# A backward FFT's blocks turned by TensorE or by DMA: two of seven blocks change sides

## The chip, the cores and the metric

The kernel runs on one core of one Trainium2 chip. The metric is the time of one execution on the device in microseconds (us), as the median of several runs. A core has a matrix engine (PE), a vector engine (DVE), a scalar engine (ACT), a general engine (POOL), a queue engine that issues transfers (SP), and 16 DMA engines that carry the transfers out.

## The reference, shortened

A network of four layers and all its gradients: two long-convolution layers (A), each followed by a dense layer with a silu (B). The vector-Jacobian product gives nine outputs: the result and the gradients of A_q, A_k, A_v, A_shift_k, A_ssm_k, A_ssm_D, B_w1 and B_w2.

```
def _A_ref(q, k, v, shift_k, ssm_k, ssm_D):          # S = 2048, D = 448
    k_shift = sum of k shifted by 0..3 rows, times shift_k
    kv = k_shift * v
    y = irfft(rfft(kv padded to 2S) * rfft(ssm_k padded to 2S))[:S]
    return q * (y + kv * ssm_D)

def _B_ref(x, w1, w2):                               # F = 1792
    return silu(x @ w1) @ w2

x = A_q
x = x + _A_ref(_layernorm(x), k, v, shift_k, ssm_k, ssm_D)
x = x + _B_ref(_layernorm(x), w1, w2)
x = x + _A_ref(_layernorm(x), k, v, shift_k, ssm_k, ssm_D)
x = x + _B_ref(_layernorm(x), w1, w2)
# outputs: x, and the gradients of the eight inputs named above, for grad_out
```

Both A layers share k, v and the filter, so the gradient of the convolution's output, summed over the two layers, goes through one FFT. Its product with the spectrum of the filter leads to the gradients of k, v and shift_k, and its product with the spectrum of kv to those of ssm_k and ssm_D.

## The kernel before

**Stages.** A prefix (`_ssm_prefix`) computes the spectra of the filter and of kv and the convolution's output y. The main part (`Main.run`) walks over four chunks of 512 rows and runs both dense layers forward and backward. The suffix (`_ssm_suffix`, from about 510 us) takes the summed gradient through the FFT and back.

**The FFT in two stages.** A length of 4096 is split into 128 by 16 by two parts. Stage 1 (`_s1_gy`, `_fft_stage1`, L218) multiplies with a table for each of 16 residues n2 and casts the result into `A1g`, 128 partitions (frequencies) by 14336 columns (channel pairs, real and imaginary part, n2). Stage 2 needs those columns on the partitions. So `A1g`, seen as `A1f` with 112 tiles of 128 x 128, is turned tile by tile into `B1v`, in seven blocks `Z[0]` to `Z[6]` of 16 tiles (2048 columns) each. This is the loop that the change touches.

**How a block is turned before.** For each of its 16 tiles, `_turn64` makes two transposes on TensorE (L225), one for each half of 64 partitions, into a bank `ps_tr` of the two PSUM banks with the tag "mm". Then one copy of 128 x 2048 brings the block to `Z[g]`; `bal.pick` gives it to ACT (L116) or DVE (L117), by the load that it has booked on each. After each block `jobs.run(1)` puts in four matmuls of the jobs.

**The jobs.** The gradients of w1 and w2 are products over all 2048 rows: 28 column blocks (14 of each), each with two groups of 16 matmuls (`ps_d`, L1046), one for each dense layer. Their stationary operands were written to memory by the main part (`a_d`, `g_d`) and come back by `Jobs.load` (L1038): one transfer of 512 KB on SP's queue for each group into `dstat`, which has four slots. `Jobs.run(n)` takes n steps of four matmuls. The jobs are spread over the suffix by hand, so that TensorE has work beside the FFT. `jobs.last_ld` is the load issued last as the program is written down.

**What follows the loop.** `spectrum(cp)` runs stage 2 (L236) over block cp, casts the result back over `Z[cp]` (L1199) and copies it with its halves swapped (L276). `inverse(cp)` multiplies with the two spectra, which `spec_load` brings by POOL's queue (L1180, L1181; tiles `kk_d` and `wts`), runs the inverse stage 2 (L265) and writes over `A1g` (as `B1k`) and over `B1v`. Steps are in the order spectrum 0, spectrum 1, inverse 0, spectrum 2, and so on. Then come the inverse stage 1 (L1271, L1300) and the sums for k, v and shift_k (L1257 to L1262, L1322, L1325).

**What sets the order.** TensorE's order is that of the program (`manual_schedule`). On the other engines and queues a scheduler places the instructions; `tc.issue_after(x)` asks that what is inside stands behind x. SP's queue issues strictly in its order: a transfer that waits holds up all behind it.

**Transposes by DMA already there.** `dma_start_transpose` turns on the way. In the prefix it turns two of seven blocks of the filter's first stage (L426, from `KAB` to `KAB`), and weights (L436, L437). In the main part it turns the jobs' operands before they are stored (L595, tile `turned`, 16 or 12 tiles at a time).

Of the kernel before, what the change touches and what calls it, by code (L numbers as in the profile page):

```python
# [11 lines left out]
BF16 = mybir.dt.bfloat16  # L12
# [5 lines left out]
P = 128  # L18
# [95 lines left out]
def _copy(nc, eng, out, in_):  # L114
    if eng is nc.scalar:
        return nc.scalar.copy(out, in_)  # L116
    return eng.tensor_copy(out, in_)  # L117
# [18 lines left out]
def kernel(  # L136
# [63 lines left out]
    with tc.manual_schedule(engines={nc.tensor.engine}):  # L200
        with ExitStack() as es:
            Main(k, es).run(ys)
        _ssm_suffix(k)
# [18 lines left out]
def _turn64(k, pt, i, src):  # L222
    for r in range(2):
        rs = slice(64 * r, 64 * r + 64)
        k.nc.tensor.transpose(pt[:, r, i, :], src[rs], k.ident[rs, rs])  # L225
# [920 lines left out]
def _ssm_suffix(k):  # L1146
    nc, tc, bal = k.nc, k.tc, k.bal
    jobs = k.jobs
    k_pm = _pm(k.A_k[0])
    v_pm = _pm(k.A_v[0])  # L1150
    psum = k.psum
    mm = dict(tag="mm", bufs=2)
    k.pt = dict(s1=mm, s2=mm, v=mm)
    A1 = k.A1g
    with ExitStack() as es:
# [12 lines left out]
        Z = [B1v_[:, 16 * g:16 * g + 16, :] for g in range(7)]  # L1168
# [3 lines left out]
        A1f = A1[:].rearrange("p a c n s -> p (a c n s)").rearrange("p (a b) -> p a b", b=P)  # L1172

        def spec_load(cp):
            lo, hi = cp * 2048, (cp + 1) * 2048
            if cp % 2:
                kk = [kk1[:, i] for i in range(2)]
            else:
                kk = [sp.tile([P, 2048], BF16, name="kk_d", tag="gK", bufs=2)[:] for i in range(2)]
            nc.gpsimd.dma_start(out=kk[0], in_=k.SPEC_d["K"][:, lo:hi])  # L1180
            k.last_sp = nc.gpsimd.dma_start(out=kk[1], in_=k.SPEC_d["KV"][:, lo:hi])  # L1181
            return kk

        kks = [spec_load(0)]
        for g in range(7):
            pt = psum.tile([P, 2, 16, 64], BF16, name="ps_tr", **mm)
            for i in range(16):
                _turn64(k, pt, i, A1f[:, 16 * g + i, :])
            _copy(nc, bal.pick(2048, dve_ns=0.53), Z[g].rearrange("p i (r x) -> p r i x", r=2), pt[:])
            jobs.run(1)  # L1190
        kks.append(spec_load(1))

        def spectrum(cp):
# [181 lines left out]
```

## Time and profile before

| what | value |
|---|---|
| three runs | 702.48 us median (701.94 to 702.93) |
| the profiled execution | 701.8 us, its span 700.0 us |
| PE busy in the span | 666.0 us (95%) |
| DVE, ACT, POOL busy | 484.1, 432.9, 101.3 us |
| granted PE clock, mean | 0.998 |
| seven blocks turned, L225 | 224 transposes, 515.7 to 524.7 us, 190 ns each (they overlap) |
| their copies | four on DVE at 1224 ns, three on ACT at 1866 ns |
| job loads, L1038 | 56 of 512 KB, median 5.2 us from issue to landing |

The span is the time from the first to the last instruction of the profiled execution, 1.8 us less than its time. Busy time of PE is a sum over matmuls that are pipelined. "Idle before" names the time for which an engine stood ahead of an instruction, and the work that ended the wait. A chain of waits is the work that ended last, followed back from the end; where it stays on one engine without a pause, that engine sets the time there.

### The profile page before, as it was taken

The page shows a single profiled execution, that of the slowest core. Times are in us where ns is not written, and L with a number is a line of the kernel's source. Part 1 is how long each engine was busy: PE and PEld are TensorE (multiplying, and loading weights), DVE is VectorE, ACT ScalarE, POOL GpSimd, SP SyncE. Part 2 cuts the span into 40 slices and gives each one's busy share as a digit, 9 for nine tenths or more (in the row PEclk, how much of TensorE's full clock was granted, in tenths as well). Part 3 has the DMA queues.
Part 4 walks back from the last instruction along what each step waited for, and adds up shares of the span by engine and source line. Part 5 has one row for each costly group of instructions (what it writes and reads, how often), then busy time and mean ns, then how long its engine had stood idle before and what let it go on. Part 6 is the DMA issues. An engine that isn't in the chain of part 4 may idle for free.

```text
span 700.0 us, 14553 instructions
## 1 busy us (share of the span) xinstructions
PE 666.0 (95%) x5897; PEld 358.8 (51%) x5933; DVE 484.1 (69%) x1131; ACT 432.9 (62%) x522; POOL 101.3 (14%) x173
## 2 busy tenths in 40 slices
PE   6898789999999999999999999999999999999996
PEld 5876545454444444434444444544554555555664
DVE  6688862676889948899578874853946545538991
ACT  5888766968856857769577585223554553554431
POOL 1057110110011100111000100010111211102311
PEclk9999999999999999999999999999999999999999
DMA  8999938459899976698677799959557888966981
GB/s 321 270 298 306 376 84 210 118 107 243 219 231 249 246 200 166 146 240 221 185 165 194 194 242 329 262 172 229 177 208 280 307 279 307 352 188 215 331 293 42
DMA packets 199798, 161.03 MB, mean 230 GB/s; under 512 B 147698, under 2 KB 180213, under 8 KB 198963
## 3 DMA queue, kind: packets, MB, share of 16 engines
q1 hardware_dynamic: 184550, 111.78, 58.8%
q0 software_dynamic: 10368, 36.29, 15.3%
q10 hardware_dynamic: 4812, 12.04, 5.0%
q8 instruction: 46, 0.75, 0.4%
q14 instruction: 22, 0.17, 0.1%
HBM read 66.05 MB, written 54.60 MB: 172 GB/s over the span
## 4 chain that ended last, share of the span: by engine, by line
PE 57%; DVE 22%; issue 10%; ACT 5%; POOL 3%; DMA 2%; POOLq 0%; DVEq 0%; ACTq 0%
PE ps_d L1046 19%; PE ps_n L836 8%; PE ps_h L638 6%; PE ps_g L638 6%; PE ps_o L798 5%; DVE ln_st L301 2%; DVE lb_v L994 2%; PE ps_v L265 2%; PE ps_cv L449 2%; POOL rstd L306 2%; DVE n L309 1%; DVE lb_v L997 1%; DVE lb_v L998 1%; DVE X L802 1%; PE ps_h L642 1%
## 5 line engine op out<-in xcount | busy, mean ns | idle before, releaser
L1046 PEld LDWEIGHTS <-dstat 128*128 128x128 bf16 x896 | 84.0, 98 | 77.8 <-issue 4.0
L836 PE MATMUL ps_n<-w1T,ghT 128*128 128x448 bf16 x448 | 96.6, 353 | 2.0 <-DVE ghT L821 1.7
L798 PE MATMUL ps_o<-w2sb,aT 128*128 128x448 bf16 x448 | 89.2, 353 | 0.7 <-DVE X L802 0.7
L638 PE MATMUL ps_h<-nT,w1sb 128*128 128x512 bf16 (+1 forms) x410 | 83.5, 336 | 2.2 <-ACT Dall L116 1.0
L116 ACT CAST ghT<-ps_g 128x1024 bf16<-128x1024 f32 (+1 forms) x54 | 48.4, 899 | 58.4 <-PE ps_g L642 47.7
L638 PE MATMUL ps_g<-nT,w2T 128*128 128x512 bf16 x317 | 77.9, 379 | 2.2 <-DVE Dall L117 0.5
L836 PEld LDWEIGHTS <-ghT 128*128 128x128 bf16 x448 | 41.4, 98 | 50.7 <-DVE ghT L821 6.7
L798 PEld LDWEIGHTS <-aT 128*128 128x128 bf16 x448 | 43.2, 98 | 41.1 <-issue 2.8
L638 PEld LDWEIGHTS <-w1sb 128*128 128x128 bf16 x420 | 39.2, 98 | 36.7 <-issue 7.2
L781 ACT ACTIVATE aT<-ps_h 128x1024 bf16<-128x1024 f32 (+1 forms) x48 | 44.2, 921 | 19.4 <-PE ps_h L638 10.5
L116 ACT CAST Dall<-ps_h 128x1024 bf16<-128x1024 f32 (+2 forms) x60 | 54.3, 904 | 0.0
L994 DVE SCALAR_TENSOR_TENSOR lb_v<-lb_u,n 128x448 bf16<-128x448 bf16 x60 | 37.2, 620 | 24.6 <-ACT lb_u L840 24.1
L791 ACT ACTIVATE Dall<-Dall 128x1024 bf16<-128x1024 bf16 (+1 forms) x48 | 53.2, 1186 | 0.1
L638 PEld LDWEIGHTS <-w2T 128*128 128x128 bf16 x336 | 31.3, 98 | 42.1 <-issue 7.2
L306 POOL TENSOR_TENSOR rstd<-ln_ve,mhalf 128x2 f32<-128x2 f32 (+1 forms) x24 | 19.9, 831 | 221.1 <-DVE ln_ve L305 221.1
L1046 PE MATMUL ps_d<-X,dstat 128*128 128x448 bf16 x224 | 47.9, 353 | 0.0
L1046 PE MATMUL ps_d<-go,dstat 128*128 128x448 bf16 x224 | 47.2, 353 | 0.0
L1046 PE MATMUL ps_d<-n3m,dstat 128*128 128x448 bf16 x224 | 46.4, 353 | 0.0
L1046 PE MATMUL ps_d<-n1m,dstat 128*128 128x448 bf16 x224 | 46.3, 353 | 0.0
L840 ACT ACTIVATE lb_u<-ps_n,rstd 128x448 bf16<-128x448 f32 x32 | 20.5, 640 | 28.7 <-PE ps_n L836 24.3
L116 ACT CAST A1g<-ps_v 128x1024 bf16<-128x1024 f32 x14 | 14.9, 1066 | 36.5 <-PE ps_v L265 36.5
L802 DVE TENSOR_TENSOR X<-X,ps_o 128x448 bf16<-128x448 bf16 x32 | 19.5, 610 | 21.3 <-PE ps_o L798 21.1
(206 smaller groups left out, 1111.6 us busy)
## 6 DMA issues: line engine op xcount, KB each, us to landing
dstat<-a_d SPq DMA_DIRECT2D x28, 512.0 KB, 5.0
dstat<-g_d SPq DMA_DIRECT2D x28, 512.0 KB, 5.2
a_d<-turned SPq DMA_DIRECT2D x16, 512.0 KB, 3.0
g_d<-turned SPq DMA_DIRECT2D x16, 512.0 KB, 3.2
a_d<-turned SPq DMA_DIRECT2D x16, 384.0 KB, 2.7
g_d<-turned SPq DMA_DIRECT2D x16, 384.0 KB, 3.0
spec_K<-KAB POOLq DMA_DIRECT2D x7, 512.0 KB, 5.4
KAB<-KAB POOLq DMA_DIRECT2D x28, 128.0 KB, 4.6
```

The source lines that it names most:

```text
L116: return nc.scalar.copy(out, in_)
L265: nc.tensor.matmul(pv[:, r ^ (ci & 1), i, :], lhsT=src[ri, i * P:(i + 1) * P], rhs=k.Gsb[ri, g, ri], start=first, stop=not first)
L306: nc.gpsimd.tensor_tensor(out=r[:, lo:hi], in0=ve[:, lo:hi], in1=k.mhalf[:, lo:hi], op=ALU.pow)
L638: self.nc.tensor.matmul(ps, lhsT=w[:, b, ft * P:(ft + 1) * P], rhs=x[:, b], start=(start and b == 0), stop=(stop and b == bs[2]))
L781: self.last_silu = nc.scalar.activation(aT[hh][:, o:o + hi - lo, :], ps(lo, hi), ACT.Silu)
L791: self.nc.scalar.activation(dT[hh][:, o:o + n, :], dT[hh][:, o:o + n, :], ACT.Derivative_silu)
L798: nc.tensor.matmul(po[:, :D], lhsT=aT[ft // 7][:, ft % 7, tl * P:(tl + 1) * P], rhs=self.w2sb[:, ft, :], start=(ft == 0), stop=(ft == NF - 1))
L802: self.last_o = nc.vector.tensor_tensor(out=X[:, t, :], in0=X[:, t, :], in1=po[:, :D], op=ALU.add)
L836: nc.tensor.matmul(pn[:, :D], lhsT=gh[ft // 7][:, ft % 7, tl * P:(tl + 1) * P], rhs=self.w1T[:, ft, :], start=(ft == 0), stop=(ft == NF - 1))
L840: nc.scalar.activation(u0[:], pn[:, :D], ACT.Identity, scale=k.rstd[2 * L + 1][:, t:t + 1], accum_out=cp[:, tl, 0:1])
L994: nc.vector.scalar_tensor_tensor(out=v[:], in0=u0, scalar=-1.0 / D, in1=n_t, op0=ALU.mult, op1=ALU.mult, accum_out=cp[:, 1:2])
L1046: self.nc.tensor.matmul(ps[:, :D], lhsT=st[:, t, :], rhs=mov[:, t, :], start=(first and t == 0), stop=(last and t == NT - 1))
```

## The change

Blocks 0 to 4 are turned by TensorE as before. Blocks 5 and 6 are turned by one DMA transpose each, on SP's queue, straight from `A1g` to `B1v`, without a PSUM bank and without a copy. Block 5's is written ahead of the loop. Block 6's is written behind the fourth step of the loop, inside an `issue_after` on the job load written down last. The seven calls of `jobs.run(1)` stay. Nothing else of the kernel is changed.

```
+        def turn_dma(g):
+            nc.sync.dma_start_transpose(out=Z[g], in_=A1f[:, 16 * g:16 * g + 16, :].rearrange("p a b -> p (a b)"))
+
+        turn_dma(5)
         for g in range(7):
-            pt = psum.tile([P, 2, 16, 64], BF16, name="ps_tr", **mm)
-            for i in range(16):
-                _turn64(k, pt, i, A1f[:, 16 * g + i, :])
-            _copy(nc, bal.pick(2048, dve_ns=0.53), Z[g].rearrange("p i (r x) -> p r i x", r=2), pt[:])
+            if g < 5:
+                pt = psum.tile([P, 2, 16, 64], BF16, name="ps_tr", **mm)
+                for i in range(16):
+                    _turn64(k, pt, i, A1f[:, 16 * g + i, :])
+                _copy(nc, bal.pick(2048, dve_ns=0.53), Z[g].rearrange("p i (r x) -> p r i x", r=2), pt[:])
             jobs.run(1)
+            if g == 3:
+                with tc.issue_after(jobs.last_ld.ins):
+                    turn_dma(6)
         kks.append(spec_load(1))
```

## The prediction

> **What bounds the kernel now.** I read the windows table first, by stages around the edit. Columns: window, its length, busy time (and instructions) of PE, PEld, DVE, ACT, POOL, then the granted clock, DMA share and GB/s.
>
> ```profile
> 515.00:529.00 14.00, 14.00 (x279) 7.62 (x278) 4.97 (x5) 7.48 (x7) 0.79 (x2) 1.00 0.49 173
> 529.00:600.00 71.00, 71.00 (x923) 38.33 (x921) 42.61 (x66) 33.05 (x39) 12.72 (x20) 1.00 0.86 308
> 633.00:660.00 27.00, 27.00 (x190) 15.78 (x189) 26.23 (x40) 12.14 (x18) 8.88 (x15) 1.00 0.81 265
> 660.00:680.00 20.00, 20.00 (x169) 12.78 (x168) 20.00 (x28) 8.76 (x15) 4.15 (x7) 1.00 0.97 343
> ```
>
> PE is busy in all of each window, the edit's own (515 to 529) among them, at full granted clock: the job matmuls (ps_d, L1046) fill every gap, so PE time taken out moves everything behind it up. In the edit's window DVE has 4.97 us of work and ACT 7.48 of 14, so the copies that go with the turns bound nothing. DVE is full as well from 660 to 680; that is a rival below.
>
> Second, the chain of waits through the edit (start, length, work):
>
> ```profile
> 520.03 0.57 PE ps_tr L225 x32
> 520.60 0.86 PE ps_d L1046 x4
> 521.47 0.57 PE ps_tr L225 x32
> 522.04 0.86 PE ps_d L1046 x4
> 522.90 0.57 PE ps_tr L225 x32
> 523.48 0.86 PE ps_d L1046 x4
> 524.34 0.57 PE ps_tr L225 x32
> ...
> 527.85 3.13 PE ps_d L1046 x16
> ...
> 531.53 6.16 PE ps_d L1046 x32
> ```
>
> The chain stays on PE here, without a wait: one block's 32 small transposes, four job matmuls, the next block.
>
> Third, the timeline, for what stands before and behind the two new transfers (start, length, engine, line, work, idle time before and its releaser):
>
> ```profile
> 514.29 0.94 ACT L116 CAST A1g<-ps_s 128x896 bf16<-128x896 f32 x1
> 515.65 0.64 PE L225 MATMUL ps_tr<-ident,A1g 64*128 64x64 bf16 x32
> ...
> 518.62 0.32 SPq L1038 DMA_DIRECT2D dstat<-a_d  x1
> 524.37 0.32 SPq L1038 DMA_DIRECT2D dstat<-a_d  x1
> ...
> 532.23 3.19 PE L1046 MATMUL ps_d<-go,dstat 128*128 128x448 bf16 x16
> ...
> 538.32 1.07 ACT L116 CAST A1g<-ps_v 128x1024 bf16<-128x1024 f32 x1 [4.33 <-PE ps_v L265]
> ```
>
> A1g is complete at 515.23 (514.29 + 0.94). The job load issued at 518.62 refills the slot of the group that has just ended (the last `go` matmuls before 518.6). There are four slots, so it is first read four groups later: X from 519.10, go from 524.85, X from 528.54, then the go group at 532.23.
>
> Last, the DMA rows for transposes of just this size (128 rows by 2048 columns) and for job loads: what, and us from issue to landing; for the second row, ns that the queue held each (least/median/most).
>
> ```profile
> turned<-ghT SPq DMA_TRANSPOSE x1, 5.5
> L426 SPq DMA_TRANSPOSE KAB<-KAB x2: 3603/4920/6238, 20.2 to 26.5; - x2
> KAB<-KAB SPq DMA_TRANSPOSE x1, 10.4
> DMA to landing us min/median/max: 3.4/5.2/11.2
> ```
>
> The first row is the 16-tile transpose issued at 482.72, the third the first of the two in the prefix, and the last stands for all 56 job loads (L1038).
>
> **The change, part by part.**
>
> *Removed on PE: blocks 5 and 6.* A block with its four matmuls starts every 1.437 us ((524.27 - 515.65) / 6 in the timeline). Four job matmuls undisturbed take (6.16 - 3.13) / 16 x 4 = 0.757 us. So a block costs 0.68 us, and two cost **1.36 us**. From above: the busy row of 0.64 plus the 0.10 by which the four matmuls behind a turn are longer (0.86 against 0.757) gives 0.74, or 1.48 for two. I take 1.36 since it is the distance between starts. All of it is on the path.
>
> *Removed on DVE and ACT:* one copy of 1.22 us (DVE) and one of 1.87 us (ACT). Neither engine bounds the window: nothing gained. The load balancer's later choices are the same in the changed program; every later engine order is the same but for these rows.
>
> *Moved forward:* PE's first spectrum matmul (L236 at 527.22) comes 1.36 us sooner. It needs block 0, copied by 517.6, and the two "mm" banks, whose last users are now block 3 (DVE copy from 520.64, 1.23) and block 4 (ACT copy from 522.08, 1.87, done at 523.95). All are done before 525.9: no wait.
>
> *Added on SP: two transposes, next to each other.* The label says the second stands behind a job's load. The load meant is the one issued at 505.91 for the group that starts at 519.10; in the changed program's SP queue the loads of 510.07 and 513.86 come next, then both transposes, then the load of 518.62. The first transpose waits for the last cast into A1g (515.23) and for stores that read the memory B1v now takes, the latest being out_dram<-g of POOL at 509.82, landed about 3 us later. No load is due on SP between 513.86 and 518.62, so nothing stands behind that wait.
>
> *What the transposes hold up.* The pair at 482.72 held SP for 4.95 us, so here SP would be free at 515.3 + 5.0 = 520.3 and the load of 518.62 issues 1.7 us late. The second transpose, issued at about 518.7, lands at about 524.2 with 5.5 us; the load behind it lands at about 524.2 + 3.4 = 527.6 even if nothing of the two overlaps. PE now wants it at 532.23 - 1.36 = 530.87: 3.2 us to spare, **cost 0**. The other end is the prefix pair: 6.24 us of queue, so the second is issued at 521.5, lands at 531.9 (10.4), the load at 535.3, and PE stands for 4.4 us. The prefix pair ran behind some MB of input loads in its own queue (v_n lands 14.5 us after its issue), whereas here the DMA share is 0.67 from 516 to 520 and 0.31 from 520 to 524. The pair at 482.72 is the nearer row, since it ran among job loads like these, at a share of 1.08. The next load (524.37, now 523.7) is wanted three us after the first and has the same room.
>
> The Trainium skill ("VectorE: DVE Perf Modes", section "The three transpose paths" and the rules after it) speaks against the edit: a 128x128 transpose goes to TensorE where PSUM will do, with 390 ns there against 1309 ns by DMA. By that figure, 16 tiles one after the other are an estimated 20.9 us a block; the trace disagrees, with 5.5 us for 16 tiles above and 0.64 us on PE.
>
> *Readers of the result.* Blocks 5 and 6 are first read by the spectrum steps of chunks 5 and 6, after 580: cover of over 50 us. The first writer over A1g is the cast at 538.32, now 536.96; it now waits for both transposes to have read it, 12 us after 524.2, and even the dear end (531.9) is earlier. The kk_d loads on POOL's queue (issued 510.62 and 511.60, landing after 6.3 and 6.8) are wanted by DVE at 528.92, now 527.6: some 9 us of cover against sharing with the transposes.
>
> *Sum.* 700.0 - 1.36 + 0 = 698.6 us of span. The profiled execution took 701.8; the median shown is 702.48, 0.68 above it, so **701.1 us**, 0.19% less.
>
> **The rivals.**
>
> *Slower: the job loads starve.* Place: SP's ring between 515.3 and the go group at 530.87. For it: the prefix rows; transposes of this size have held the queue for 6.24 us. Against it: the shares, and PE busy in full (5.60 of 5.60) during the pair at 482.72. Price at the dear end 4.4 - 1.36 = 3.0, so 705.5. It decides once that load lands after 530.87, and the kernel is slower from 532.23 on.
>
> *Given back at the tail: DVE.* For it: DVE is full from 660 to 680.
>
> ```profile
> 630.63 0.62 DVE L1274 TENSOR_TENSOR gks<-gkv,gks 128x896 bf16<-128x896 bf16 x1 [7.77 <-ACT gkv L1273]
> 683.35 0.19 DVE L1325 SCALAR_TENSOR_TENSOR skjunk<-ps_sk,mask 128x32 bf16<-128x32 f32 x1 [0.97 <-PE ps_sk L1322]
> ```
>
> That chain begins after 7.77 us of idleness, on a cast that follows PE, so it moves up with PE; at its end DVE waits another 0.97 for PE. Were it not to move at all, 1.36 - 0.97 = 0.39 would be lost at most: 701.5.
>
> *The transposes run tile after tile.* The mechanism: a transpose's tiles serialise at twice the dear end's 10.4 us or more, so the load behind the second lands after 515.3 + 41.6 + 3.4 = 560.3 and PE stands for 29 us: 730. No transpose of the trace supports it; the larger ones of w2T land in 11.7 (median of two). The page above would put it there (41.9 us for two blocks by its figure, an estimate).
>
> *It doesn't do what it says.* The second transpose isn't held back as the label has it (above). As no load sits between, that costs nothing by itself and belongs to the forecast.
>
> **How the numbers follow.** Forecast 0.76; starved loads 0.16; tail 0.06; tile after tile 0.02. What a measurement of this kernel can tell from no change is about 0.2%, 1.4 us, and the forecast's 1.36 to 1.48 straddles it; I put 0.50 of its 0.76 beyond the line, since what the readings leave out can only add to the gain (in the timeline most turns show 0.37 us of issue idle before their first weight load, 0.7 for two, which overlaps the matmuls before it and is counted at nothing), and 0.26 within. With the tail within: faster 0.50, same 0.32, slower 0.18. The likeliest case's own range is 700.5 to 701.7 (a gain of 2.0 with those gaps, and of 0.8 if a load is a little late). For 8 in 10 it reaches toward the tail and a part of the starved case, up to a full give-back: 700.4 to 702.6.
>
> **What would show it.** Right: 64 fewer L225 transposes of A1g, the first L236 at about 525.9, PE full from 515 to 692, two transposes on SP at 515 to 519 landing by 525, the load behind them by 528. Wrong: PE idle ahead of the go group near 531 with a dstat load as the releaser; ACT's cast into A1g near 537 waiting for a transfer; PE earlier at 526 but not at 692.

## The result, and the profile after

The changed kernel takes 701.65 us in the median of 22 runs, the kernel before 702.87 us in 22 runs beside it: 1.2 us less, a ratio of 0.9983 (95% interval 0.9976 to 0.9990). Two later comparisons on the chip gave 0.9968 (0.9953 to 0.9984) and 0.9986 (0.9977 to 0.9994). So the change is worth 0.1 to 0.3%, about what such a comparison can just tell from nothing.

The profiled execution has a span of 699.5 us, against 700.0. That 0.5 is no measure of the change: in this execution the first turn of the loop starts at 516.46, 0.81 us later than before (515.65), and nothing ahead of it was changed. In the executions profiled for this study that start lies anywhere between 515.50 and 519.26. So I measure from the loop's first turn onward, where the three profiles of the changed kernel agree to a few hundredths (the kernel before has one profile). The windows of the changed kernel, with columns as before; they end 1.4 us sooner than those before, each on its own execution's clock:

```profile
515.00:527.60 12.60, 12.60 (x215) 6.67 (x213) 3.67 (x3) 5.48 (x6) 1.10 (x2) 1.00 1.09 258
527.60:598.60 71.00, 71.00 (x922) 38.42 (x921) 42.67 (x66) 33.94 (x40) 12.18 (x20) 1.00 0.87 311
658.60:678.60 20.00, 20.00 (x178) 13.00 (x176) 20.00 (x28) 9.29 (x16) 4.17 (x7) 1.00 0.97 337
```

PE is still busy in all of each window at full clock. The DMA share in the edit's window has gone from 0.49 to 1.09: the transfers fill what was half empty. The chain of waits through the edit (start, length, work):

```profile
521.41 0.86 PE ps_d L1046 x4
522.28 0.57 PE ps_tr L225 x32
522.85 3.89 PE ps_d L1046 x20
526.74 0.56 PE ps_s L236 x8
527.30 3.13 PE ps_d L1046 x16
```

The last turn is now followed by 20 job matmuls in one piece, with the two turns gone from between them, and then by the first spectrum matmuls. From the timelines: first turn to first spectrum matmul 526.67 - 516.46 = 10.21 us, before 527.22 - 515.65 = 11.57. That is 1.36 us. First turn to the last matmul of the program (ps_r, which starts at 694.38 and before at 694.89): 177.92 against 179.24. So 1.32 of the 1.36 is still there at the end.

What the transfers did, first in the timeline of the changed kernel:

```profile
516.11 7.43 SPq L1186 DMA_TRANSPOSE B1v<-A1g  x2
...
523.66 0.51 SPq L1038 DMA_DIRECT2D dstat<-a_d  x1
...
531.68 3.19 PE L1046 MATMUL ps_d<-go,dstat 128*128 128x448 bf16 x16
```

Then by their line: ns for which the queue held each (least/median/most), the first and last start, and us to landing:

```profile
L1186 SPq DMA_TRANSPOSE B1v<-A1g x2: 3212/3690/4167, 516.1 to 520.3; - x2
...
DMA to landing us min/median/max: 6.7/7.1/7.6
```

And in the list of transfers the two job loads behind them, with their landing in us:

```profile
dstat<-a_d SPq DMA_DIRECT2D x2, 512.0 KB, 4.9
```

The pair holds SP until 523.54. The job load that stood at 518.62 before, so at 519.43 on this execution's clock, issues at 523.66, 4.2 us late. The 4.9 us are those of the second load of the two alone, issued at 524.50 and landed at 529.4; the list has no landing for the first. Its semaphore in the trace, which counts 16 updates for a transfer, has the last of them at 528.12. PE reads this load at 531.68: 3.6 us to spare, and no wait. In the two other profiles of the changed kernel it issues 5.7 us late and has 2.5 us to spare by the same reading.

### The profile page after: what moved, and what is told of

The parts are those of the page before. It is cut to its first block, busy times and chain, and to the rows that moved or that the text cites. A ratio compares the mean times of both kernels' runs of the same rounds, so it can differ in the third digit from the quotient of the medians.

```text
span 699.5 us, 14467 instructions
## 1 busy us (share of the span) xinstructions
PE 670.4 (96%) x5869; PEld 360.7 (52%) x5869; DVE 483.1 (69%) x1130; ACT 431.3 (62%) x521; POOL 101.6 (15%) x173
## 4 chain that ended last, share of the span: by engine, by line
PE 59%; DVE 19%; issue 10%; ACT 5%; POOL 4%; DMA 2%; POOLq 0%; DVEq 0%; ACTq 0%
PE ps_d L1046 19%; PE ps_n L836 9%; PE ps_h L638 7%; PE ps_o L798 6%; PE ps_g L638 6%; DVE ln_st L301 2%; PE ps_v L265 2%; POOL rstd L306 2%; DVE lb_v L994 2%; PE ps_h L642 2%; DVE X L802 1%; ACT Dall L116 1%; DVE n L309 1%; PE ps_g L642 1%; DVE lb_v L997 1%
## 5 line engine op out<-in xcount | busy, mean ns | idle before, releaser
L638 PE MATMUL ps_g<-nT,w2T 128*128 128x512 bf16 x336 | 79.5, 379 | 1.0 <-DVE Dall L117 0.5
```

Of the source, the lines that this page charges most:

```text
L638: self.nc.tensor.matmul(ps, lhsT=w[:, b, ft * P:(ft + 1) * P], rhs=x[:, b], start=(start and b == 0), stop=(stop and b == bs[2]))
```

## The experiments

All are edits of the changed kernel. Times by part are differences of starts in each kernel's own timeline, as above. "Wait" is PE's wait for a job load between the loop and the end.

| kernel | blocks by DMA | first turn to first spectrum matmul | first turn to last ps_r | PE's wait | time over before (95% interval) |
|---|---|---|---|---|---|
| before | 0 | 11.57 | 179.24 | 0 | 1 |
| changed, three profiles | 2 | 10.21, 10.21, 10.20 | 177.92, 177.90, 177.89 | 0 | 0.9983, 0.9968, 0.9986 |
| one block | 1 | 10.89 | 178.59 | 0 | 0.9993 (0.9981 to 1.0006) |
| no transfer | 0, two left out | 10.21 | 177.91 | 0 | 0.9966 (0.9952 to 0.9980) |
| each twice | 2 | 10.20 | 181.62 | 1.9 | 1.0031 (1.0015 to 1.0047) |
| three adjacent | 3 | 9.53 | 177.67 | 0.3 | 0.9988 (0.9972 to 1.0004) |
| three spread | 3 | 9.53 | 178.00 | 0.6 | 0.9962 (0.9945 to 0.9980) |
| three interleaved, twice | 3 | 9.53, 9.53 | 177.22, 177.20 | 0 | 0.9970 (0.9956 to 0.9983), 0.9975 (0.9967 to 0.9984) |
| four interleaved | 4 | 8.85 | 183.56 | 4.4 | 1.0040 (1.0020 to 1.0059) |
| four, n3m later | 4 | 8.84 | 176.53 | 0 | 0.9969 (0.9957 to 0.9981) |

Most of these ratios overlap; the verdicts below rest on the parts.

**The changed kernel again.** 

> The changed kernel itself, beside the other three on one chip. Expected: from the first turn (L225) to the first spectrum matmul (L236) 10.21 us as in its first profile, against 11.57 before; time 1.2 to 1.4 us under the kernel before. A theory in which the gain is only the scatter of the runs expects no difference from before (under 0.3 us).

The parts came out as expected. The ratio 0.9968 was larger than expected and the third comparison smaller again: the runs scatter by more than the effect.

**No transfer.** The two transfers become fills by POOL.

```
-            nc.sync.dma_start_transpose(out=Z[g], in_=A1f[:, 16 * g:16 * g + 16, :].rearrange("p a b -> p (a b)"))
+            nc.gpsimd.memset(Z[g], 0.0)
```

> Leaves out the turning of blocks 5 and 6: POOL fills them with zeros, and no transfer takes the place of TensorE's work. Theory (the two transfers cost nothing, since the job load behind them still lands some 3 us before PE reads it): the same time as the changed kernel, within 0.4 us, and 10.21 us from the first turn to the first spectrum matmul. Rival (the transfers cost something by sharing the DMA engines or by moving loads): faster than the changed kernel by 0.5 us or more.

177.91 against 177.89 to 177.92, and 701.46 us beside 701.36 for the changed kernel: two transfers there cost nothing that can be seen. The whole gain comes from what was taken away. That this is PE's turns and not the copies follows from the chain, which stays on PE without a wait in both kernels.

**One block.** Only block 6 goes to DMA.

```
-        turn_dma(5)
+        turn_dma(6)
-            if g < 5:
+            if g < 6:
-            if g == 3:
-                with tc.issue_after(jobs.last_ld.ins):
-                    turn_dma(6)
```

> Only block 6 goes to DMA; block 5 is back on TensorE. Theory (0.68 us a block, nothing else): 10.89 us from the first turn to the first spectrum matmul, and 178.57 from the first turn to the last ps_r matmul, against 179.24 before and 177.9 with two blocks. Rival (the gain comes from the freed copies or PSUM banks of the last two blocks): not half of it, but all or none.

10.89 and 178.59, as the theory has it: 0.68 for the first block and 0.68 for the second. The rival, all or none, falls. A share that goes with each block's own copy would be halved here as well, so against that only the chain without a wait speaks. In time the one block can't be told from nothing.

**Each block twice.** Behind `turn_dma(6)` stand `turn_dma(5)` and `turn_dma(6)` once more.

> TensorE's work as in the changed kernel; each of the two blocks is turned by DMA twice, four transfers in a row (5, 6, 5, 6) ahead of the same job load, with the same result. Theory (the load behind the transfers has some 3 us to spare, and from there each us of SP is a us of PE): by the holds measured so far (3.2 to 4.9 us each) SP is free 12.7 to 16 us after the first turn, the load lands 5 us later, and PE waits 2 to 5 us for it near 531. The kernel is 2 to 5 us slower than the changed one, so 1 to 4 us slower than before. Rival (transfers on SP are hidden anyway, as no cost was seen with none against two): same as the changed kernel within 0.4 us.

The four hold SP for 13.21 us, the load issues at 531.01, and PE stands for 1.9 us. But the part up to the last ps_r grew by 181.62 - 177.91 = 3.7 us, twice the wait. The timeline and then the windows of this kernel (columns as above; the granted clock is the third from the end) tell why:

```profile
535.29 4.88 PE L1046 MATMUL ps_d<-go,dstat 128*128 128x448 bf16 x16 [1.86 <-DMA dstat<-a_d]
```

```profile
533.30:535.30 2.00, 0.14 (x2) 0.01 (x1) 1.96 (x5) 1.72 (x3) 0.00 (x0) 1.00 0.94 344
...
536.00:538.00 2.00, 2.00 (x7) 0.81 (x6) 1.96 (x3) 0.00 (x0) 0.00 (x0) 0.50 1.12 443
...
540.00:542.00 2.00, 2.00 (x12) 1.07 (x11) 0.00 (x0) 0.00 (x0) 0.35 (x1) 1.00 1.01 423
```

Right behind the wait the granted clock is 0.50, and full again by 540. The 16 matmuls behind the wait took 4.88 us, against 3.19 for the same group in the changed kernel: 1.7 us more. Wait and slow clock together make 3.6 of the 3.7 us. The theory holds in its direction, and the rival (hidden anyway) falls; the price of a us late was put too low for this execution. It took 706.60 us, and the median of the ten runs is 705.48; whether the clock dipped in the others too is not known.

**Three blocks, adjacent and spread.** Block 4 by DMA too, first right behind the other two, then behind the job load that they hold up.

```
-            if g < 5:
+            if g < 4:
                     turn_dma(6)
+                    turn_dma(4)                          # adjacent
...
+            if cp == 0:                                  # spread: after spectrum(1), ahead of inverse(0)
+                with tc.issue_after(jobs.last_ld.ins):
+                    turn_dma(4)
```

> Block 4 goes to DMA too, its transfer right behind the other two, all ahead of the same job load. Theory (SP's queue is the price): three transfers hold SP for 3 x 3.7 = 11.1 us, so on the time axis of the changed kernel's profile the load issues at 527.3 and lands at 532.2 at the earliest, while PE, 0.68 us sooner, wants it at 531.0: PE waits 1.2 us there, and the kernel is 0.5 us slower than the changed one. Rival (each block moved is worth 0.68 us whatever stands on the queue): 0.7 us faster than the changed kernel, no wait of PE.

> Block 4 goes to DMA too, but its transfer stands behind the job load that the other two hold up. Theory (the place in the queue decides): the load issues at about 523.7 and lands by 529, PE never waits, and the kernel is 0.7 us faster than the changed one, 2.0 us faster than before. Rival (the DMA engines' share is the price, wherever the transfer stands): the loads land late here as well, and it is no faster than with three adjacent.

Adjacent, the three held SP for 9.52 us rather than 11.1, and PE waited 0.3 rather than 1.2. The wait is there, as the theory has it, but too small to use up the third block's gain: the part is 0.2 us under the changed kernel's, where 0.5 over was expected. Spread, the theory missed: the wait was longer, and the part is 0.1 over the changed kernel's, where 0.7 under was expected. The timeline of the spread form, and from its list of transfers the load issued at 531.21:

```profile
525.71 5.39 SPq L1186 DMA_TRANSPOSE B1v<-A1g  x1
...
535.40 2.44 PE L1046 MATMUL ps_d<-X,dstat 128*128 128x448 bf16 x12 [0.60 <-DMA dstat<-a_d]
```

```profile
dstat<-a_d SPq DMA_DIRECT2D x1, 512.0 KB, 4.1
```

The first load was in time, but the third transfer held SP from 525.71 to 531.10. So the second load issued only at 531.21 and landed 4.1 us later, at 535.3, where PE had stood for 0.6 us. I had followed one load and not the next. Both the first theory, with only one load in view, and its rival, that three are too many wherever they stand, are answered by the next experiment.

**Three blocks, interleaved.** One transfer ahead of each of three job loads: 5, load, 6, load, 4, load. `if g < 4` stands here too; the second piece below is from `inverse`, which is written ahead of the first.

```
-            if g == 3:
-                with tc.issue_after(jobs.last_ld.ins):
-                    turn_dma(6)
...
+            if cp == 0:                                  # after spectrum(1)
+                with tc.issue_after(jobs.last_ld.ins):
+                    turn_dma(6)
...
                 jobs.run(6 - u)
+                if cp == 0 and u == 0:
+                    with tc.issue_after(jobs.last_ld.ins):
+                        turn_dma(4)
```

> Blocks 5, 6 and 4 by DMA, one transfer ahead of each of three job loads in turn, so that no load stands behind more than one. Theory (what counts is how late each load lands against its own group): load 1 issues near 520.4 and is wanted at 531, load 2 near 525 and wanted at 534, load 3 near 530 and wanted at 538; PE waits for none, 177.2 us from the first turn to the last ps_r, 0.7 faster than the changed kernel. Rival (three transfers are too many for the DMA engines wherever they stand): a wait of 0.3 to 0.6 us as with the two other forms of three.

No wait, and 177.22 where 177.2 was expected. Against it the waits of 0.3 and 0.6 us in the two other forms of three cost 0.45 and 0.78. The transfers held SP for 4.0 to 4.7 us each, landed after 6.1 to 8.2, and cost nothing. In another comparison:

> Three interleaved blocks beside the next form on one chip: 177.2 us from the first turn to the last ps_r, 0.7 over the form with four if that has no wait.

177.20, and 701.31 us against 701.81 for the changed kernel in the same comparison.

**Four blocks, interleaved.** `turn_dma(3)` behind `turn_dma(4)`, and `if g < 3`.

> As with three interleaved, and block 3 by DMA too, its transfer behind that of block 4, ahead of load 3. Theory: load 3 issues near 534 and lands near 539, wanted at 537.5, so PE waits about 1.5 us and the fourth block's 0.68 us is more than given back: 178.0 us from the first turn to the last ps_r. Rival (0.68 for each block): 176.5.

The stall came, and later and far larger: 4.4 us at a load further on, and a part of 183.56, 5.65 us over the changed kernel. The load that was expected to be late landed 4.1 us after its issue, in time for its group. The one that stalled PE stands behind the n3m transfer (1.8 MB), which SP's order has between the two. With three interleaved, the load in this place (issued at 531.88) took 9.0 us and was still in time. The timeline, the load issued at 533.32 in the list of transfers, and a window:

```profile
532.82 0.38 SPq L1107 DMA_DIRECT2D n3m<-N_d  x1
533.32 0.35 SPq L1038 DMA_DIRECT2D dstat<-a_d  x1
...
545.23 3.17 PE L1046 MATMUL ps_d<-X,dstat 128*128 128x448 bf16 x8 [4.44 <-DMA dstat<-a_d]
```

```profile
dstat<-a_d SPq DMA_DIRECT2D x1, 512.0 KB, 11.9
```

```profile
545.00:547.00 2.00, 1.77 (x5) 0.73 (x6) 0.00 (x0) 0.00 (x0) 0.35 (x1) 0.50 1.03 416
```

Issue at 533.32 plus 11.9 is 545.22, and PE goes on at 545.23. The clock behind it is 0.50 again, here until about 550.

**Four blocks, with n3m a chunk later.** n3m is first read near 577, so its transfer can wait.

```
-            if cp == 0:
+            if cp == 1:
                 with tc.issue_after(jobs.last_ld.ins):
                     jobs.load_n3()
```

> Four blocks by DMA, interleaved as before, but the transfer of n3m (1.8 MB, first used near 577) goes onto SP one chunk later, behind five more job loads. Theory (the 4.4 us stall with four came from one job load that shared the DMA engines with n3m, landing 12.9 us after its issue, and the dip of the clock behind it): that load lands 5 to 6 us after its issue near 533, wanted near 541; no wait of PE, and 176.5 us from the first turn to the last ps_r, 1.4 faster than the changed kernel. Rival (four transfers are too many for SP or for the DMA engines): a wait of PE of over 1 us near 541 remains.

(The 12.9 us there is the median of that load and the next; the load itself took 11.9.) The same load, the one for the X group that now starts at 541.28, is issued at 532.57 in this form; from the list of transfers:

```profile
dstat<-a_d SPq DMA_DIRECT2D x1, 512.0 KB, 5.1
```

No wait is left and the part is 176.53: four blocks at (179.24 - 176.53) / 4 = 0.68 us each. The rival falls. This form beats both kernels in the parts, by 2.7 us and by 1.4; in time it took 700.54 us in five runs, beside 701.81 for the changed kernel and 702.87 for the one before, a ratio to before of 0.9969 (0.9957 to 0.9981). The interval holds the 0.9961 that the part alone gives.

## The prediction, step by step

- **0.68 us for a block, all on the path: right.** 1.36 between the first turn and the first spectrum matmul; one, three and four blocks gave 0.68 each too. The distance between starts was the right reading; the 0.74 made of busy rows was not.
- **The copies on DVE and ACT are worth nothing: right**, by the chain, which never leaves PE there, and by the size: the gain is the distance between PE's starts, block by block. No run took a copy away alone.
- **The second transfer has no load between it and the first: right.** The timeline has both in one piece.
- **SP's hold: too short, by a wrong reading.** I took 4.95 us for the pair, from the pair at 482.72. But only the first of that pair has 16 tiles; the second has 12, as the 384 KB of its store show. The timeline before, taken apart:

```profile
482.72 3.39 SPq L595 DMA_TRANSPOSE turned<-ghT  x1
486.27 1.39 SPq L595 DMA_TRANSPOSE turned<-ghT  x1
```

Twice 3.39 would have been 6.8. The new pair held SP for 7.43, 8.86 and 8.90 in the three profiles of the changed kernel, 3.2 to 5.0 each. The load issued 4.2 us late in the first of them and 5.7 in the others, rather than 1.7. Landing took 6.7 to 8.3 rather than 5.5.

- **3.2 us to spare, cost 0: right**, at 3.6, 2.5 and 2.5, but in part by luck. I let the load land 3.4 us after the second transfer. In all three profiles it landed 1.1 us after it (in the first 520.33 + 6.67 = 527.00, against 528.12). Two errors in opposite directions nearly cancelled.
- **The tail on DVE gives nothing back: right**, 1.32 of 1.36 arrive. DVE's chain moved up with PE. From the first turn it begins after 630.12 - 516.46 = 113.66 us, before 114.98, and DVE waits for PE at its end as long as before:

```profile
630.12 0.62 DVE L1282 TENSOR_TENSOR gks<-gkv,gks 128x896 bf16<-128x896 bf16 x1 [7.80 <-ACT gkv L1281]
...
682.84 0.19 DVE L1333 SCALAR_TENSOR_TENSOR skjunk<-ps_sk,mask 128x32 bf16<-128x32 f32 x1 [0.97 <-PE ps_sk L1330]
```

- **Starved loads, the rival on the other side:** the mechanism is real and begins just behind what the change does. Two transfers more turned the gain into a loss. Its price was put too low: I took a us of wait for a us of time, and in the execution profiled it was nearly two.
- **Tile after tile, the rival: not borne out.** Transposes of 16 tiles landed in 4.3 to 8.3 us in all runs here. Twice two transfers held up PE by 1.9 us and not by tens.
- **In time** 1.2 us measured against 1.4 forecast. The forecast of 701.1 stood on a median before of 702.48 from three runs; over 22 runs it is 702.87. The runs of either kernel spread over 3 us or more, so the size is settled by the parts alone.

## What to carry to other kernels

Where the matrix engine is never idle, look at the distance between starts for what a piece of its work is worth: two rows of the timeline give it, and here it held from one block to four. What takes its place on a queue is free only as long as each later load on that queue still lands ahead of its own reader, so follow all of them, one by one, big transfers between them too, not only the first. Spreading the new transfers one by one between the loads, and moving a large transfer that isn't needed yet, made room for twice as many.

## What was not expected of the hardware

A short wait of PE can cost more than its length. Waits of 0.3 and 0.6 us left the granted clock at 1.00, while one of 1.9 us was followed by about 3.4 us at 0.50 (535.7 to 539.1), and one of 4.4 us by a clock of 0.50 from about 543.9, still within the wait, to about 550.6. So 1.9 us became 3.7, and 4.4 became 183.56 - 176.53 = 7.0. But the dip does not come each time. Near 82 us every profile here has a PE gap of 2.45 us, with PE waiting for DVE, and in four of the 13 (the first and third of the changed kernel, one block, each twice) 3.4 us at 0.50 come with it; in the other nine the clock stays at 1.00 there. What decides it is not shown, and the 1.9 and 4.4 us are one execution each. The Trainium skill ("TensorE: Matmul & The Clock Gate", the rules "Why this matters for your kernels") warns of PE-idle gaps over about 3 us; here 1.9 and 2.45 us were enough in some executions. The length of these dips is like the window of 3.4 us that the same page of the Trainium skill gives (section "What's actually happening").

One of the new transposes of 16 tiles held SP's queue for 2.0 to 5.4 us in these runs, where a job load of the same bytes held it for 0.3 to 0.5 in most cases.
